# A causal convolution and soft mixture on one core: maxima of the taps carried by 32-column matmuls, and taken earlier

## Chip, core and metric

The kernel runs on one core of one Trainium2 chip. The metric is the device time of one execution in microseconds, lower is better. All data are float32.

## What is computed

The input is `x` (8 sequences of 3584 tokens, 192 channels in 8 heads of 24) and, for each token and head, 7 tap weights. The first half is a causal convolution whose 7 taps are a softmax of those weights; the second a soft mixture of 8 experts with 4 slots each.

```python
w = weight_gen - np.max(weight_gen, axis=-1, keepdims=True)     # (B, S, H, 7)
w = np.exp(w); w = w / (np.sum(w, axis=-1, keepdims=True) + 1e-09)
x_unf = x_pad[:, idx, :].reshape(B, S, K, H, group)              # 7 rows of x per token
out = np.einsum('bshk,bskhg->bshg', w, x_unf)                    # convolution
logits = out @ phi                                               # 28672 tokens x 32 slots
d = softmax of logits over the tokens;  slot_input = d.T @ out
slot_out[e] = np.maximum(slot_input[e] @ w1[e], 0.0) @ w2[e]
y = (softmax of logits over the slots) @ slot_out
```

## The kernel before

A sequence is cut into 35 groups of 104 tokens: 4 blocks of 26 tokens. Seven groups make a stage `s` (40 stages), two groups a pair `p` (140 pairs), eight pairs a unit `u`. PE, DVE, ACT and POOL each run their instructions in the order in which the kernel writes them; the main loop gives each step a planned moment (`at(t, step, ...)`), sorts by it and writes the steps in that order. `start[p]` is pair p's planned begin, with CONV = 0.8, XPOSE = 0.46, ROWS = 0.5, LOGITS = 1.5 and DISPATCH = 0.75 as planned lengths. SP issues the loads in the same list.

The steps of a pair, with the lines of the profile:

- `conv(p)`, L223, PE: 16 matmuls of 26 stationary columns (a banded matrix of taps) by 100 moving columns of x. The four blocks of a group write to four bands of 32 output partitions of one of three buffers `cv`. A float32 matmul stands in the trace as two MATMUL and two LDWEIGHTS records.
- `conv_sum` (L232, ACT) and `conv_out` (L239 reciprocal and L240 multiply, DVE) divide by the sum of the taps and write `tm`.
- `xpose(p - 3)`, L253, PE: three transposes, copied out by ACT (L258).

The steps of a stage's taps, seven pairs ahead of the stage's first convolution, in four stages' buffers `taps`:

- `tap_top(s)`, L176, DVE: maximum over the 7 taps, from 128 x 392 to 128 x 56. It waits for the load of `taps` (L169).
- `tap_rows(s)`, L182, PE: carries these maxima to the rows of x at which the taps stand. For each of the 7 tap positions q, one matmul with the 128 x 128 matrix `sel[:, q]` as stationary operand and the 128 x 56 maxima as the moving one. `sel[:, q]` links only rows and columns of the same head, that is, it has four blocks of 32 x 32. The result goes to `topP`, a part of the PSUM tile `pmx`.
- `tap_sub` (L186, DVE), `tap_exp` (L190, ACT) and `band_make` (L199, POOL, four instructions) subtract, exponentiate and lay out the banded matrices.

The steps of a unit: `logits` (L282, PE), `top` and `save` (L289, L291, L295, DVE), `newmax` (L304, PE; it writes another part of `pmx`), `newmax_out` (L309, L311, DVE), `dexp` (L315, ACT), `dturn` (L327, DVE), `dispatch` (L347, PE) and `rescale` (L355, DVE). The softmax over slots (L77 to L90) runs beside them on DVE, POOL and ACT. After the loop come the experts and the output matmuls (L609 to L670).

Stages 0 to 2 have their taps prepared in a hand-written part ahead of the loop; the other 37 in the loop.

Of the kernel before, what the change touches and what calls it, by code (L numbers as in the profile page):

```python
# [41 lines left out]
def conv_soft_moe(ctx, tc, xh, wh, phi, w1a, w1b, w2, out):  # L42
    nc = tc.nc
    V, A, G, P, SY = nc.vector, nc.scalar, nc.gpsimd, nc.tensor, nc.sync
# [72 lines left out]
    topP = pmx[:, 0:TAPS].rearrange("p (q l) -> p q l", q=KT)  # L117
# [30 lines left out]
    sel = keep.tile([128, KT, 128], F32, name="sel")  # L148
# [22 lines left out]
    tops = {}  # L171
# [7 lines left out]
    def tap_rows(s):  # L179

        for q in range(KT):
            P.matmul(topP[:, q], sel[:, q], tops[s][:, :, 0], start=True, stop=True)  # L182

    def tap_sub(s):
        r = taps[s % NTAP][:, 1].rearrange("p (b q o) -> p q b o", q=KT, o=2)
# [164 lines left out]
    def rescale(u):  # L350
# [3 lines left out]
        else:  # L354
# [13 lines left out]
                    op=ALU.mult)  # L368
    tap_top(0)
    tap_rows(0)  # L370
    for q in range(4):
        r = slice(32 * q, 32 * q + 32)
# [20 lines left out]
    for t in tms:  # L393
        V.memset(t[:, :, 0:1], 1.0)
        V.memset(t[:, :, 2 * D + 1 : 2 * D + 2], 1.0)
    conv(0)
    tap_rows(1)
    conv_sum(0)
    conv_out(0)
# [15 lines left out]
    conv_out(1)  # L415
    tap_top(2)
    tap_rows(2)
    tap_sub(2)
    tap_exp(2)
    band_make(2, 0, 14)  # L420
    band_make(2, 14, HB)
    for q in range(4):
        r = slice(32 * q, 32 * q + 32)
# [24 lines left out]
    start = [0.0]  # L448
# [7 lines left out]
    def at(t, f, *a):  # L456
        todo.append((t, len(todo), f, a))

    for p in range(first, PAIRS):
        t = start[p]  # L460
        at(t, conv, p)
        at(t + CONV + 0.1, conv_sum, p)
        at(t + CONV + 0.4, conv_out, p)
        if p >= LAG:
            at(t + CONV, xpose, p - LAG)
            at(t + CONV + XPOSE + 0.05, xpose_out, p - LAG)
        t += CONV + XPOSE
        if p in rowed:
            s = rowed[p]
            at(t - 1.2, tap_top, s)  # L470
            at(t, tap_rows, s)
            t += ROWS
            at(t + 0.1, tap_sub, s)
            at(t + 0.7, tap_exp, s)
            at(t + 1.4, band_make, s, 0, 14)
            at(t + 3.4, band_make, s, 14, HB)
    saved = {}
    for u in range(1, final + 1):
        v, p0 = u - 1, UNITS[u][0]
        t = start[p0 + LAG + 1] - LOGITS  # L480
# [5 lines left out]
        if u < final:  # L486
            t = start[p0 + LAG + 2] - 0.01
# [5 lines left out]
            t = start[p0 + UP] - DISPATCH  # L493
            at(t, dispatch, v)
            at(t + DISPATCH + 0.2, rescale, v)
    for h in range(2 * EARLY):
        t = saved[(sum(HALVES[h]) - 1) // (2 * UP)] + 1.5
# [3 lines left out]
    for s in range(NSG):  # L501
        for part in range(2):
            g = SGG * s + (SGH, SGG)[part] - 1
            t = start[g // 2] + CONV * (0.5, 1)[g % 2] + 0.01
# [97 lines left out]
    for i in range(E + E // 2):  # L602
        for q in range(4):
            r = slice(F // 4 * q, F // 4 * (q + 1))
# [32 lines left out]
    for e in range(E):  # L637
        for c in range(FC):
            q = c % 4
            P.matmul(so4[32 * q : 32 * q + 32], hT[:, c, NS * e : NS * e + NS],  # L640
                     w2_at(e, q * 2 + c // 4),
                     start=(e == 0 and c < 4), stop=(e == E - 1 and c >= 4))
# [132 lines left out]
```

## Time and profile before

| | |
|---|---|
| median of 3 runs | 432.2 us (428.71 to 448.68) |
| profiled execution | 427.8 us |
| its span, first to last instruction | 426.1 us |
| mean granted TensorE clock | 0.918 |
| PE busy (matmul records) | 378.1 us, 89% of the span |
| DVE, POOL, ACT busy | 267.6, 180.7, 164.0 us |

A line of the profile names the engine, the source line, the operation, the tiles written and read, and the number of instructions. PE is the matmul stream and PEld the weight loads; they overlap. In the timeline the first column is the start in us, the second the length of the merged piece, and brackets give the idle time ahead of it and what ended it. The ends of matmuls are modelled, so lengths hold a fixed tail of about a quarter of a microsecond.

### The profile page before, as it was taken

The page shows a single profiled execution, that of the slowest core. Times are in us where ns is not written, and L with a number is a line of the kernel's source. Part 1 is how long each engine was busy: PE and PEld are TensorE (multiplying, and loading weights), DVE is VectorE, ACT ScalarE, POOL GpSimd, SP SyncE. Part 2 cuts the span into 40 slices and gives each one's busy share as a digit, 9 for nine tenths or more (in the row PEclk, how much of TensorE's full clock was granted, in tenths as well). Part 3 has the DMA queues.
Part 4 walks back from the last instruction along what each step waited for, and adds up shares of the span by engine and source line. Part 5 has one row for each costly group of instructions (what it writes and reads, how often), then busy time and mean ns, then how long its engine had stood idle before and what let it go on. Part 6 is the DMA issues. An engine that isn't in the chain of part 4 may idle for free.

```text
span 426.1 us, 16874 instructions
## 1 busy us (share of the span) xinstructions
PE 378.1 (89%) x7184; PEld 283.5 (67%) x7184; DVE 267.6 (63%) x631; ACT 164.0 (38%) x424; POOL 180.7 (42%) x206
## 2 busy tenths in 40 slices
PE   7589999989999998989989999998989998998940
PEld 7577777867777786777868778786767665323310
DVE  5636657655766766676776766676676754877440
ACT  4224334333434434343443434434344412543420
POOL 3435454545635654653755653564753243000000
PEclk9569999979999999999999999999999999995555
DMA  5626888883464653355464464555453690699996
GB/s 149 176 75 185 269 248 233 262 253 108 137 171 120 156 166 108 108 152 167 123 175 129 113 186 132 137 143 152 113 147 94 234 361 3 266 399 401 400 398 240
DMA packets 31131, 80.85 MB, mean 190 GB/s; under 512 B 6864, under 2 KB 6992, under 8 KB 31056
## 3 DMA queue, kind: packets, MB, share of 16 engines
q1 hardware_dynamic: 31056, 79.77, 59.8%
q8 instruction: 57, 0.93, 0.9%
q14 instruction: 18, 0.15, 0.1%
HBM read 57.38 MB, written 22.36 MB: 187 GB/s over the span
## 4 chain that ended last, share of the span: by engine, by line
PE 59%; DVE 22%; DMA 6%; ACT 4%; issue 3%; SPq 2%; DVEq 0%; POOL 0%; ACTq 0%; POOLq 0%
PE pmx L182 17%; PE cv L223 15%; PE pt L253 7%; PE ls L282 7%; DVE tm L240 6%; PE ac L347 6%; DMA out<-big 6%; DVE top L176 3%; PE po L661 2%; DVE ws L239 2%; SPq L670 2%; DVE mx L289 2%; DVE LT L295 2%; ACT dd L315 2%; PE hp L609 1%
## 5 line engine op out<-in xcount | busy, mean ns | idle before, releaser
L199 POOL TENSOR_TENSOR band<-taps,mask 128x140 f32<-128x140 f32 (+2 forms) x156 | 137.8, 913 | 120.1 <-issue 91.7
L223 PE MATMUL cv<-big,band 128*26 128x100 f32 x4480 | 128.1, 255 | 3.5 <-POOL band L199 3.5
L223 PEld LDWEIGHTS cv<-big,band 128*26 128x26 f32 x4480 | 100.1, 107 | 18.6 <-issue 8.4
L182 PE MATMUL pmx<-top,sel 128*128 128x56 f32 x560 | 74.6, 288 | 20.7 <-DVE top L176 18.3
L182 PEld LDWEIGHTS pmx<-top,sel 128*128 128x128 f32 x560 | 69.8, 202 | 28.2 <-DVE top L176 24.9
L240 DVE TENSOR_TENSOR tm<-cv,ws 128x384 f32<-128x384 f32 x140 | 78.2, 559 | 15.0 <-PE pmx L182 0.5
L253 PE MATMUL pt<-ident,tm 122*128 122x122 f32 x420 | 74.9, 288 | 0.0
L258 ACT COPY cm<-pt 128x312 f32<-128x312 f32 x140 | 58.2, 417 | 13.8 <-PE pt L253 12.9
L239 DVE RECIPROCAL ws<-ws 128x16 f32<-128x16 f32 x140 | 33.6, 240 | 40.6 <-ACT ws L232 39.2
L253 PEld LDWEIGHTS pt<-ident,tm 122*128 122x128 f32 x420 | 43.3, 142 | 22.1 <-issue 20.1
L232 ACT ACTIVATE ws<-cv,eps 128x16 f32<-128x16 f32 x140 | 37.5, 268 | 52.5 <-PE cv L223 51.6
L190 ACT ACTIVATE taps<-taps 128x392 f32<-128x392 f32 x40 | 21.2, 530 | 90.8 <-DVE taps L186 90.8
L661 PE MATMUL po<-cT,so 32*128 32x442 f32 (+3 forms) x256 | 44.8, 771 | 2.8 <-DVE big L668 2.0
L186 DVE TENSOR_TENSOR taps<-taps,pmx 128x392 f32<-128x392 f32 x40 | 22.5, 563 | 35.9 <-PE pmx L182 33.0
L668 DVE COPY big<-po 128x936 f32<-128x936 f32 (+1 forms) x24 | 26.1, 1094 | 16.4 <-DMA out<-big 9.0
L661 PEld LDWEIGHTS po<-cT,so 32*128 32x128 f32 (+1 forms) x256 | 15.6, 199 | 30.8 <-ACT big L668 12.6
L668 ACT COPY big<-po 128x936 f32<-128x936 f32 (+1 forms) x24 | 21.8, 917 | 32.1 <-DMA out<-big 11.3
L79 POOL TENSOR_TENSOR LT<-LT,rm 128x576 f32<-128x576 f32 (+1 forms) x16 | 18.0, 1130 | 36.6 <-DVE rm L77 33.3
L282 PE MATMUL ls<-cm,phi_sb 128*32 128x208 f32 (+1 forms) x576 | 28.4, 336 | 0.9 <-ACT cm L258 0.9
L347 PE MATMUL ac<-tm,dt 128*32 128x193 f32 x544 | 28.0, 349 | 1.2 <-DVE dt L327 1.2
L90 POOL TENSOR_TENSOR LT<-LT,sm 128x576 f32<-128x576 f32 (+1 forms) x16 | 18.1, 1132 | 11.9 <-DVE sm L88 7.6
L282 PEld LDWEIGHTS ls<-cm,phi_sb 128*32 128x32 f32 x576 | 16.5, 109 | 8.2 <-ACT ws L232 1.3
(112 smaller groups left out, 245.2 us busy)
## 6 DMA issues: line engine op xcount, KB each, us to landing
big<-xh SPq DMA_DIRECT2D x160, 100.0 KB, 2.5
taps<-wh SPq DMA_DIRECT2D x40, 392.0 KB, 4.1
big<-xh SPq DMA_DIRECT2D x160, 75.0 KB, 3.3
out<-big SPq DMA_DIRECT2D x24, 468.0 KB, 6.4
out<-big SPq DMA_DIRECT2D x24, 442.0 KB, 6.5
big<-w SPq DMA_DIRECT2D x7, 768.0 KB, 9.1
w1a_sb<-w1a SPq DMA_DIRECT2D x8, 512.0 KB, 4.9
w1b_sb<-w1b SPq DMA_DIRECT2D x4, 512.0 KB, 6.3
```

What stands on the lines that cost most here:

```text
L182: P.matmul(topP[:, q], sel[:, q], tops[s][:, :, 0], start=True, stop=True)
L199: eng.tensor_tensor(out=w[:, :, z].rearrange("p b (a k) -> p b a k", k=k), in0=r[:, :, :, 0:k].to_broadcast([128, hi - lo, a, k]), in1=m[: ...
L223: P.matmul(cv[32 * blk : 32 * blk + T, o : o + 4 * GX], bands[s % NBAND][:, bc // 2, :, bc % 2], xb[:, :, bc * GX : (bc + 1) * GX], start= ...
L232: A.activation(wss[p], cvs[p % NCV][:, 0 : 16 * GX].rearrange("p (h w) -> p h w", w=GX)[:, :, GW:], AF.Identity, bias=eps[:, 0:1])
L239: V.reciprocal(ws, ws)
L240: V.tensor_tensor(out=tms[u % NTM][:, pr, 1 : 2 * D + 1].rearrange("p (h w) -> p h w", w=GW), in0=cv[:, :, 0:GW], in1=ws.to_broadcast([128 ...
L253: P.transpose(pt[:, i, 0:TR], tm[0:TR, pr, 1 + 128 * i : 129 + 128 * i], ident[0:TR, 0:TR])
L258: copy(cms[u][:, pr].rearrange("p i b j -> p (i b) j"), pts.pop(p).rearrange("p i (b j) -> p (i b) j", j=32)[:, :, 0:T])
L282: P.matmul(lp[32 * blk : 32 * blk + 32, 0:n, par, 0:T], phi_sb[:, 2 * par + i, :], cm[:, 0:n, 1 if i else 2 * par, blk, :], start=(i == 0) ...
L347: P.matmul(ac[32 * q : 32 * q + 32], dt[:, g, :], tm[:, g // 2, o : o + D + 1], start=(g < 4), stop=(g + 4 >= 2 * n))
L661: P.matmul(po[dst : dst + hi - lo, q % 2, 0 : n * T], so[32 * q : 32 * q + 32, lo:hi], cT[32 * q : 32 * q + 32, g0 : g0 + n, 0:T], start=T ...
L668: (V.tensor_copy if done[1] % 2 else A.copy)(ot.rearrange("p (q c) -> p q c", q=2), po[:, :, 0 : n * T])
```

## The change

Each matmul of `tap_rows` becomes four, one for each 32 columns of `sel[:, q]`, each writing its own band of 32 partitions of `topP`; all four still read all 128 rows and the same moving operand. In the loop, `tap_top` is planned 2.5 ahead of `tap_rows` instead of 1.2.

```diff
     def tap_rows(s):
         for q in range(KT):
-            P.matmul(topP[:, q], sel[:, q], tops[s][:, :, 0], start=True, stop=True)
+            for r in range(0, 128, 32):
+                P.matmul(topP[r : r + 32, q], sel[:, q, r : r + 32], tops[s][:, :, 0],
+                         start=True, stop=True)
...
         if p in rowed:
             s = rowed[p]
-            at(t - 1.2, tap_top, s)
+            at(t - 2.5, tap_top, s)
             at(t, tap_rows, s)
             t += ROWS
             at(t + 0.1, tap_sub, s)
```

The orders of ACT, POOL and SP are the same in both, as is that of PE but for the count of the matmuls. On PE, at stage 20, these stand in a row before:

```order
L182 MATMUL pmx_98<-top20_2625,sel_138 128x56 x7
L347 MATMUL ac6_2645<-tm0_91,dt6_2604 32x193 x16
L223 MATMUL cv1_95<-big_67,band0_88 26x100 x16
L253 MATMUL pt61_2686<-ident_132,tm1_92 128x122 x3
L223 MATMUL cv2_96<-big_67,band0_88 26x100 x16
```

and now (the lines of the changed kernel are one or two higher):

```order
L183 MATMUL pmx_98<-top20_3007,sel_138 32x56 x28
L349 MATMUL ac6_3086<-tm0_91,dt6_3026 32x193 x16
L225 MATMUL cv1_95<-big_67,band0_88 26x100 x16
L255 MATMUL pt61_3127<-ident_132,tm1_92 128x122 x3
L225 MATMUL cv2_96<-big_67,band0_88 26x100 x16
```

Seven matmuls with 128 output rows have become 28 with 32, and nothing else has moved. On DVE, at the same stage (`ws`, `tm`: conv_out; `rm`: softmax over slots; `dd`, `dt`: dturn), before:

```order
L239 RECIPROCAL ws61_2567<-ws61_2567 128x16
L240 TENSOR_TENSOR tm1_92<-cv1_95,ws61_2567 128x384
L77 TENSOR_REDUCE rm5_2590<-LT_65 128x17
L322 MEMSET dd_93 64x32
L324 MEMSET dd_93 32x4
L327 STREAM_TRANSPOSE dt6_2604<-dd_93 128x512
L239 RECIPROCAL ws62_2600<-ws62_2600 128x16
L240 TENSOR_TENSOR tm1_92<-cv2_96,ws62_2600 128x384
L176 TENSOR_REDUCE top20_2625<-taps0_84 128x56
```

and now:

```order
L241 RECIPROCAL ws61_2987<-ws61_2987 128x16
L242 TENSOR_TENSOR tm1_92<-cv1_95,ws61_2987 128x384
L176 TENSOR_REDUCE top20_3007<-taps0_84 128x56
L77 TENSOR_REDUCE rm5_3012<-LT_65 128x17
L324 MEMSET dd_93 64x32
L326 MEMSET dd_93 32x4
L329 STREAM_TRANSPOSE dt6_3026<-dd_93 128x512
L241 RECIPROCAL ws62_3022<-ws62_3022 128x16
L242 TENSOR_TENSOR tm1_92<-cv2_96,ws62_3022 128x384
```

The reduce of `tap_top` has moved up six rows here, past one `conv_out` and a `dturn`. In the loop it moves up two to six rows at 33 of the 37 stages, past one `conv_out` each time and at some of them past a `dturn`, a `newmax_out`, a `top` and `save` or a `rescale` too; at four stages (10, 17, 26, 33) it stays where it was.

## Prediction

> **What bounds the kernel now.** I read the page first: busy times, and the chain that ended last by engine and by line.
>
> ```profile
> PE 378.1 (89%) x7184; PEld 283.5 (67%) x7184; DVE 267.6 (63%) x631; ACT 164.0 (38%) x424; POOL 180.7 (42%) x206
> ...
> PE 59%; DVE 22%; DMA 6%; ACT 4%; issue 3%; SPq 2%; DVEq 0%; POOL 0%; ACTq 0%; POOLq 0%
> PE pmx L182 17%; PE cv L223 15%; PE pt L253 7%; PE ls L282 7%; DVE tm L240 6%; PE ac L347 6%; DMA out<-big 6%; DVE top L176 3%; PE po L661 2%; DVE ws L239 2%; SPq L670 2%; DVE mx L289 2%; DVE LT L295 2%; ACT dd L315 2%; PE hp L609 1%
> ```
>
> The changed line, L182, has the largest share of the chain: 17% of 426.1 us, 73 us for 40 rounds of work. L176 adds 3%. Then the busy times of the loop alone, and the waits in it (total us, times, longest).
>
> ```profile
> core 0: us, PE busy (x) PEld busy (x) DVE busy (x) ACT busy (x) POOL busy (x), PEclk, DMA share, GB/s
> 20.00:333.00 313.00, 292.52 (x6293) 236.55 (x6297) 205.87 (x514) 126.36 (x369) 164.63 (x180) 0.97 0.56 156
> ```
> ```profile
> DVE ws L239 <- ACT ws L232: 36.8, 51, 2.4
> DVE taps L186 <- PE pmx L182: 25.5, 26, 2.6
> PEld pmx L182 <- DVE top L176: 21.0, 25, 2.1
> PEld pmx L182 <- DVE mq L311: 2.8, 4, 0.7
> PE ac L347 <- DVE dt L327: 1.2, 3, 0.6
> ```
>
> In the loop PE is busy 292.5 of 313 us, DVE only 205.9. Nearly all that PE waits for is the maxima: 21.0 + 2.8 = 23.8 us by the weight loads' count, at 29 of 37 stages. So time taken off PE here is time taken off the loop, until DVE stands in the way.
>
> **The matmuls.** Here is one stage without a wait, and the next pair, without taps.
>
> ```profile
> 74.22 0.54 PE L253 MATMUL pt<-ident,tm 122*128 122x122 f32 x3
> 74.49 1.64 PEld L182 LDWEIGHTS pmx<-top,sel 128*128 128x128 f32 x14
> 74.59 1.67 PE L182 MATMUL pmx<-top,sel 128*128 128x56 f32 x14
> 76.19 0.89 PE L223 MATMUL cv<-big,band 128*26 128x100 f32 x32
> ```
> ```profile
> 77.02 0.53 PE L253 MATMUL pt<-ident,tm 122*128 122x122 f32 x3
> 77.48 0.89 PE L223 MATMUL cv<-big,band 128*26 128x100 f32 x32
> ```
>
> From the transposes to the convolution it is 76.19 - 74.22 = 1.97 us with the taps and 77.48 - 77.02 = 0.46 without: they cost 1.51 us. The 14 loads follow each other at (1.64 - 0.19) / 13 = 0.112 us, while a convolution's 32 records, each with more moving columns, take 0.89 in all. So loading 128 columns sets the pace, not streaming 56. What 32 columns cost is shown by neighbours: the convolution's 32 run on four bands, and less the tail of some 0.25 its starts lie within 0.64 us, 0.020 each; eight rounds of four, so a round takes some 0.088 for 100 columns. Small loads stand further on.
>
> ```profile
> 348.00 0.14 PEld L577 LDWEIGHTS pst<-phi_sb,accS 128*32 128x32 f32 x2
> 348.17 0.20 PEld L582 LDWEIGHTS psu<-selE,accS 128*64 128x64 f32 x4
> ...
> L577 PEld LDWEIGHTS pst<-phi_sb,accS 128*32 128x32 f32 x2 | 0.1, 108 | 0.0
> ```
>
> Two loads of 32 columns on one band start 0.14 - 0.108 = 0.03 apart, and four of 64 columns on two bands fit in 0.20: bands load beside each other. The 56 new records are 14 rounds of four. A round is bounded below by the load, 0.03, if streaming cost nothing, and above by four convolution records, 0.08. The convolution's round scaled to 56 columns is 0.049, and its load is hidden, as there; I take **14 x 0.049 = 0.69 us** instead of 1.51. The change of shape after the transposes is in the 0.46 already. Over 37 stages that is 37 x 0.82 = **30.3 us**. (At four stages a 128-column matmul follows and the shape changes back; under 1 us, left out.)
>
> The three stages prepared ahead of the loop are on the chain too, the first as in the loop, two at half clock, which shows in a piece twice as long:
>
> ```profile
> 13.90 3.24 PE L182 MATMUL pmx<-top,sel 128*128 128x56 f32 x14
> ...
> 22.19 3.23 PE L182 MATMUL pmx<-top,sel 128*128 128x56 f32 x14 [3.56 <-DVE top L176]
> ```
>
> Half the clock doubles what is saved, so 0.8 + 2 x 1.6 = **4.0 us**. The wait of 3.56 us stays: that part is written by hand, and its order on DVE is unchanged.
>
> **The earlier maxima.** The longest waits look like this:
>
> ```profile
> 163.18 0.56 DVE L240 TENSOR_TENSOR tm<-cv,ws 128x384 f32<-128x384 f32 x1
> 163.65 0.71 DVE L77 TENSOR_REDUCE rm<-LT 128x17 f32<-128x544 f32 x1
> 164.20 0.53 PE L253 MATMUL pt<-ident,tm 122*128 122x122 f32 x3
> 164.53 0.71 DVE L327 STREAM_TRANSPOSE dt<-dd 128x512 f32<-128x512 f32 x1
> 165.95 0.55 DVE L176 TENSOR_REDUCE top<-taps 128x56 f32<-128x392 f32 x1
> 166.56 1.64 PEld L182 LDWEIGHTS pmx<-top,sel 128*128 128x128 f32 x14 [2.05 <-DVE top L176]
> ```
>
> Moved to behind the multiply of 163.18, the reduce ends at 164.2, before the transposes: the 2.05 us go. But L327 then ends at 164.53 + 0.71 + 0.55 = 165.8, and `dispatch`, which follows the taps and reads it, would be ready at 164.66 + 0.69 = 165.35: a new wait of 0.45. There are four such places. Elsewhere the reduce passes at least one `conv_out` (0.24 + 0.56 us of DVE), and the mean wait is 21.0 / 25 = 0.84, so most end. The reduce issues nothing but itself, and no other engine's order changes, SP's and POOL's loads and bands included. At the four "mq" waits the taps still wait for L311, which ends earlier by the 0.55 of the reduce now ahead of it; 0.2 of 0.7 stays. I leave 3 of the 23.8 us: **20.8**. What the reduce delays by 0.55 is mostly `conv_out`; its readers come three pairs later, 3 x 1.29 = 3.9 us, which covers it. Without that cover each stage would lose 0.55, 20 us in all.
>
> **New waits.** The four of 0.45 on `dt`, and the three present ones (1.2 us) grow by perhaps 0.3 each: 2.7. The moved reduce may find its load not landed, and then all of DVE stands behind it.
>
> ```profile
> DMA to landing us min/median/max: 3.0/4.1/6.1
> ```
> ```profile
> 35.34 0.35 SPq L169 DMA_DIRECT2D taps<-wh  x1
> ...
> 41.91 0.55 DVE L176 TENSOR_REDUCE top<-taps 128x56 f32<-128x392 f32 x1
> ```
>
> This is the tightest stage, 6.6 us from issue to reduce; with 0.8 from the move and 1.6 from two shorter stages 4.2 are left, a wait of up to 2 us for DVE, partly covered. I allow 1.8 in all, so **-4.5**.
>
> **The clock.** After one such wait the clock fell to half for some 6 us, after another more briefly (the first row is the same work undisturbed):
>
> ```profile
> 72.09 1.51 PE L347 MATMUL ac<-tm,dt 128*32 128x193 f32 x32
> ...
> 90.26 3.24 PE L182 MATMUL pmx<-top,sel 128*128 128x56 f32 x14 [1.80 <-DVE top L176]
> 93.43 2.80 PE L347 MATMUL ac<-tm,dt 128*32 128x193 f32 x32
> ...
> 168.26 2.34 PE L347 MATMUL ac<-tm,dt 128*32 128x193 f32 x32
> ```
>
> (3.24 - 1.67) + (2.80 - 1.51) + (2.34 - 1.51) = 3.7 us. Without the waits that should go; since two equal waits had no fall, I take **3**.
>
> **Sum.** 30.3 + 4.0 + 20.8 - 4.5 + 3 = 53.6 us. The profiled execution took 427.8 us, so **374 us**. The median of the three runs is 1% above that execution, which I put into the range.
>
> **Rivals.** (a) *Starting a matmul has a price of its own.* If a record can't start faster than in the convolution, 0.020 us, the 56 take 1.12 instead of 0.69: 40 x 0.43 = 17 us are lost, **391**. Against it: a round's length there fits streaming, as it grows with the columns (32 records of L347 with 193 columns take 1.51; less a tail of 0.34, seven rounds of 0.167 are again 0.088 per hundred columns). The Trainium skill, page "TensorE: Matmul & The Clock Gate", section "Wait — 56ns, not 53.3ns?", says that starts never come closer than about 25 ns however few the columns. By it the 56 would take an estimated 1.40 us and the kernel about 402; the 0.020 of the convolution is already below it.
>
> (b) *DVE becomes the bound.* With 48 us off the loop, DVE would be busy 206 of 265 us, 78%. If its 36.8 us of waits for ACT stay and it only gains part of its 25.5 us for the taps, the loop falls by 33 instead: **391**. For it: its order is fixed, and it waits once a pair. Against it: 107 us of idle time.
>
> (c) *Slower: bands load and stream one after another*, 0.03 + 0.049 = 0.08 us for each of 56, 4.4 us a stage: 374 + 40 x 3.7 = **522**. Other gains are 19 us, 0.48 a stage, so this decides from (1.51 + 0.48) / 56 = 0.036 us per matmul on. The Trainium skill, same page, section "The mechanism", has loads overlap running matmuls only where the row groups differ, and here all use all rows. The convolution, with the same rows, runs at 0.020: the trace disagrees.
>
> (d) *Nothing measurable*: both halves hidden. PE's 93% in the loop speaks against it.
>
> **Chances.** Forecast 0.62; (a) 0.17; (b) 0.14; (d) 0.03; (c) 0.04. The low end is all waits gone and no new ones, 427.8 - 30.3 - 4.0 - 23.8 - 3.7 = 366. A round at its lower bound, 0.03, would take 40 x 14 x 0.019 = 11 us more off; with the convolution's round so near to streaming I allow 3 of them. The high end takes in (a) and (b) and the median's 1%: 391 + 1% = 395, and 3 more for new waits a good half larger than allowed. Two per cent, 8.6 us, is about what a measurement here can tell from none. Faster by over that: 0.93; within: 0.03; slower: 0.04.
>
> **What would show it.** 2240 matmul records of `tap_rows`, a stage's busy piece near 0.9 us with its tail instead of 1.67; PE's wait for the top reduce under 4 us in the loop; that of `dispatch` for L327 near 3; DVE's wait for the taps roughly halved; the loop's clock at 0.98 or more instead of 0.97, DVE's share there near 78%. I am wrong if the piece is 1.3 us or longer, or if PE in the loop waits more than 12 us.

## The result and the profile after

The changed kernel takes 396.1 us (median of four runs, 395.57 to 397.02) where the kernel before takes 430.5 (four runs, 427.91 to 448.68) in the same session: ratio 0.922, 95% interval 0.916 to 0.929. The ratio leaves out the one execution of 448.68, which stands far from the others of the same kernel. The profiled execution took 396.47 us instead of 427.8, so 31.3 us are gone, not the 53.6 that the sum gave. The time lies inside the forecast range of 363 to 398, near its upper end.

From the page of the changed kernel: busy times, and the chain that ended last by engine and by line.

```profile
PE 344.5 (87%) x8864; PEld 246.9 (63%) x8864; DVE 265.2 (67%) x631; ACT 161.3 (41%) x424; POOL 180.7 (46%) x206
...
PE 66%; DVE 11%; DMA 9%; issue 6%; ACT 3%; SPq 1%; DVEq 0%; POOL 0%; ACTq 0%; POOLq 0%
```

Then the loop of the changed kernel by itself (columns as in the row of before: window and its length, busy times, granted clock, DMA share, GB/s), and what PE waited for there (total us, times, longest).

```profile
20.00:302.00 282.00, 261.11 (x7902) 202.25 (x7903) 201.67 (x510) 123.72 (x369) 164.01 (x179) 0.98 0.62 174
```
```profile
PE cv L225 <- issue: 15.1, 16, 2.7
PE pmx L183 <- DVE top L176: 4.5, 2, 3.9
PE ac L349 <- DVE dt L329: 1.4, 4, 0.6
PE ac L349 <- issue: 1.1, 1, 1.1
PE pmx L183 <- issue: 1.1, 3, 0.5
PE ls L284 <- issue: 0.8, 2, 0.4
```

PE's work shrank and its waits for the maxima are nearly gone (of the 4.5 us, 3.9 belong to the hand-written part), yet PE is still idle for 21 of these 282 us. The largest row is new: 15.1 us ahead of convolution matmuls, "issue", which is time in which PE waits for nothing that the profile shows. The three other "issue" rows add 3.0.

Cut at the first start of the convolution of pair 2, the loop's first, and at the last start of all, the profiled executions compare so:

| us | before | after | difference |
|---|---|---|---|
| up to the convolution of pair 2 | 25.4 | 21.0 | -4.4 |
| loop | 311.8 | 284.9 | -26.9 |
| rest | 89.0 | 88.9 | -0.1 |

**What the new idle time is.** The timeline of the changed kernel at its longest stall but one:

```profile
71.80 0.58 PE L183 MATMUL pmx<-top,sel 128*32 128x56 f32 x32
...
72.19 0.68 PE L225 MATMUL cv<-big,band 128*26 128x100 f32 x19
...
74.93 0.88 PE L225 MATMUL cv<-big,band 128*26 128x100 f32 x13 [2.06 <-issue]
75.73 0.49 PEld L255 LDWEIGHTS pt<-ident,tm 122*128 122x128 f32 x3 [0.30 <-issue]
75.73 0.87 PE L255 MATMUL pt<-ident,tm 122*128 122x122 f32 x3
...
76.53 1.55 PE L225 MATMUL cv<-big,band 128*26 128x100 f32 x32
...
78.59 0.89 PE L225 MATMUL cv<-big,band 128*26 128x100 f32 x32
```

A convolution whose operands are all there stops after 19 of its 32 records. Two microseconds later it goes on, and for some 3 us after that PE runs at half speed (transposes 0.87 instead of 0.53, a convolution 1.55 instead of 0.89). A break in the middle of a step that waits for nobody points at the instructions themselves. The queue of the page that loads instructions has more packets than before; here are the rows of before and of after:

```profile
q8 instruction: 57, 0.93, 0.9%
```
```profile
q8 instruction: 70, 1.15, 1.3%
```

Each packet is 16 KB. The trace has 14,549 PE records before and 17,910 after (matmuls, weight loads, and some semaphore instructions): one packet for 256 records in both, and 13 packets more for 3,361 records more. I numbered the records from 0 in order of start, and call the time from the start of one record to that of the next a break where it is over 0.2 us. Records 193, 449, 705 and so on lie 256 apart; I call them borders. In the loop of the changed kernel 28 breaks, 25.6 us in all, stand at borders; before there is one, of 0.35 us. So PE's code seems to come in pieces of 256 records, with PE standing at the border of one until it has arrived. The packets' own times fit: in a stall PE goes on 1.2 to 1.6 us after a packet's end. The stall above ends at 74.92; the packet ran from 72.20 to 73.45.

Leaving these breaks out, the loop is 311.8 - 0.35 = 311.4 us before and 284.9 - 25.6 = 259.3 after. The difference, 52.1, is near the 49.6 that the sum held for the loop (53.6 less the 4.0 ahead of it).

### The profile page after: what moved, and what is told of

The parts are those of the page before. It is cut to its first block, busy times and chain, and to the rows that moved or that the text cites. A ratio compares the mean times of both kernels' runs of the same rounds, so it can differ in the third digit from the quotient of the medians.

```text
span 394.8 us, 20235 instructions
## 1 busy us (share of the span) xinstructions
PE 344.5 (87%) x8864; PEld 246.9 (63%) x8864; DVE 265.2 (67%) x631; ACT 161.3 (41%) x424; POOL 180.7 (46%) x206
## 4 chain that ended last, share of the span: by engine, by line
PE 66%; DVE 11%; DMA 9%; issue 6%; ACT 3%; SPq 1%; DVEq 0%; POOL 0%; ACTq 0%; POOLq 0%
PE cv L225 24%; PE pt L255 13%; DMA out<-big 8%; PE pmx L183 8%; PE ls L284 7%; PE ac L349 6%; DVE tm L242 2%; PE po L663 2%; PE hp L611 1%; PE cv L131 1%; PE so L642 1%; DVE big L670 1%; DVE mx L291 1%; DVE LT L297 1%; ACT dd L317 1%
## 5 line engine op out<-in xcount | busy, mean ns | idle before, releaser
L225 PE MATMUL cv<-big,band 128*26 128x100 f32 x4480 | 134.3, 254 | 19.0 <-issue 15.1
L225 PEld LDWEIGHTS cv<-big,band 128*26 128x26 f32 x4480 | 103.4, 106 | 36.4 <-issue 27.7
L183 PE MATMUL pmx<-top,sel 128*32 128x56 f32 x2240 | 38.2, 218 | 5.8 <-DVE top L176 4.5
L183 PEld LDWEIGHTS pmx<-top,sel 128*32 128x32 f32 x2240 | 31.5, 112 | 13.1 <-DVE top L176 5.4
```

The source lines that it names most:

```text
L183: P.matmul(topP[r : r + 32, q], sel[:, q, r : r + 32], tops[s][:, :, 0], start=True, stop=True)
L225: P.matmul(cv[32 * blk : 32 * blk + T, o : o + 4 * GX], bands[s % NBAND][:, bc // 2, :, bc % 2], xb[:, :, bc * GX : (bc + 1) * GX], start= ...
```

## The experiments

The theory: **the code supply.** PE now gets through 256 records in less time than the next piece takes to come. The rivals are given with each run. "Breaks" below means the breaks at these borders in the loop, read from the one profiled execution of each kernel.

### The two halves apart

128 columns with the early maxima, as an edit of the kernel before:

```diff
-            at(t - 1.2, tap_top, s)
+            at(t - 2.5, tap_top, s)
```

> The earlier maxima alone, matmuls of 128 columns as before. Theory S (supply of PE's code: its records come in pieces of 256, a piece is asked for only when PE enters the one ahead of it, and PE stalls where it uses up 256 records before that comes, some 4 to 5 us): with 14,500 records as before a piece lasts some 6 us, so no stall at piece boundaries (under 2 us in all), PE's wait for the maxima under 3 us, about 405 us (428 - 21 for the waits - 4 for the clock + 2 for new waits). Rival D (what is missing of the forecast gain is held back by DVE's fixed order): the waits come back elsewhere, 413 us or more.

And four matmuls of 32 columns with the maxima at their old place, as an edit of the changed kernel:

```diff
-            at(t - 2.5, tap_top, s)
+            at(t - 1.2, tap_top, s)
```

> Four matmuls of 32 columns, maxima taken as late as before. Theory S: taps of 0.69 us a stage as in the changed kernel, waits for the maxima back at some 20 us; part of them lies over piece boundaries, during which code arrives, so stalls there fall from 25 to some 12 us: 405 us. If the two costs simply add (waits as before on top of the changed kernel), 417 us. Rival D: within 2 us of the changed kernel, 396.

Early maxima alone: 402.9 us (401.35 to 408.11), ratio 0.938 [0.932, 0.943]; breaks 1.3 us. Short matmuls alone: 410.3 (409.78 to 411.73), ratio 0.957 [0.952, 0.961]; breaks 21.1 us. PE's waits with the short matmuls alone:

```profile
PE pmx L183 <- DVE top L176: 18.7, 18, 5.0
PE cv L225 <- issue: 13.5, 15, 3.0
```

| | loop, us | breaks, us | loop without breaks |
|---|---|---|---|
| before | 311.8 | 0.35 | 311.4 |
| early maxima alone | 287.2 | 1.3 | 285.9 |
| short matmuls alone | 298.7 | 21.1 | 277.6 |
| both | 284.9 | 25.6 | 259.3 |

The early maxima alone came out near the 405 forecast for them, without stalls, so DVE's order (413 or more) isn't what holds the gain back. The stalls come with the short matmuls, also where the maxima are late. There I was wrong on their size: the waits for the maxima did not cover them, they fell to 21.1 us and not to 12, and 410.3 lies between the theory's 405 and the 417 of costs that simply add. Without the breaks the halves are worth 25.5 and 33.8 us, 59.3 together; both at once give 52.1; why they overlap by 7 us isn't shown. With the breaks the short matmuls bring 13.1 us of the loop beside late maxima and 2.3 beside early ones: nearly all they save beside the early maxima is given back at the borders.

### Half as many records

Two matmuls of 64 columns, early maxima:

```diff
-            for r in range(0, 128, 32):
+            for r in range(0, 128, 64):
-                P.matmul(topP[r : r + 32, q], sel[:, q, r : r + 32], tops[s][:, :, 0],
+                P.matmul(topP[r : r + 64, q], sel[:, q, r : r + 64], tops[s][:, :, 0],
```

> Two matmuls of 64 columns (two heads) instead of four of 32; maxima early. 56 records for a stage instead of 112, 16,000 in all. Theory S: a stage's taps take some 14 rounds of 0.056 = 0.78 us (+0.09 x 37 = 3 us), the stalls at piece boundaries fall from 25 us to under 10: 383 us, faster than the changed kernel. Rival T (the stalls come from small column tiles as such, in proportion to their number): half of them stay, 387 to 390. Rival D: 399.

387.5 us (386.62 to 388.25), ratio 0.902 [0.897, 0.908], the intervals of this and the changed kernel do not overlap. Its waits on PE, and its code:

```profile
PE pmx L183 <- DVE top L176: 5.6, 4, 4.2
PE cv L225 <- issue: 2.8, 4, 1.4
PE ls L284 <- ACT cm L260: 2.1, 3, 0.9
```
```profile
q8 instruction: 61, 1.00, 1.1%
```

A stage's taps are slower than with 32 columns: 0.81 us from first to last start instead of 0.68, and 0.15 us from the last start to the next convolution instead of 0.03. Between 64 columns and the convolution's bands the shape changes once more (behind 128 columns it is 0.21). Over 37 stages that is 4.6 + 4.5 us, which is what the loop without breaks is longer: 274.9 - 6.5 = 268.4 instead of 259.3 us. But it has 15,670 records instead of 17,910, breaks of 6.5 us instead of 25.6, and wins by 8.5 us. The time is the one that rival T had, 387 to 390, and not the theory's 383; what speaks for the theory are the breaks, of which T leaves half and the theory under 10 us. The theory's time had not counted the second change of shape.

### The border is counted in records

Sixteen matmuls of one moving column (64 records) behind the first stage's taps, into PSUM that nobody reads:

```diff
+        if s == 0:
+            for i in range(16):
+                r = i % 4 * 32
+                P.matmul(pmx[r : r + 32, 410 + i : 411 + i], sel[:, 0, r : r + 32], tops[s][:, 0:1, 0], ...
```

> The changed kernel with 16 more matmuls of one moving column behind the taps of stage 0, where PE waits for data anyway: 64 records more ahead of the loop. Theory S: PE's long stalls without a releaser stand again at record numbers 193 modulo 256, thus at other places of the program than before (64 records earlier in it); their sum stays near 20 to 26 us and the time at 394 to 398 us. If the stalls belong to places in the program, they stand at 1 modulo 256 now (193 + 64).

399.1 us (396.95 to 404.91), ratio 0.926 [0.920, 0.932], a little over the 394 to 398 expected. Every later step now stands 64 records further on. Of the breaks of over 0.4 us from 24 to 300 us, 25 with 31.0 us are still at record 193 of each 256 and 4 of under 0.6 us elsewhere; in the changed kernel 22 with 23.7 us, and 5 elsewhere. A break that belonged to a step of the kernel would have moved to 257, that is, to 1 of the next 256. Its sum is larger, 33.4 us, where 20 to 26 were expected; the profiled execution was the longest of the four, 404.91 us, so only the place is read from it.

### Is it the rate, and not the number?

The early 128-column matmuls with 21 matmuls of one moving column a stage, which stand in the trace as 42 matmuls and 42 weight loads: as many records as in the changed kernel, but no work saved. First three behind each of the seven:

```diff
             P.matmul(topP[:, q], sel[:, q], tops[s][:, :, 0], start=True, stop=True)
+            for r in range(0, 96, 32):
+                P.matmul(pmx[r : r + 32, 410 + q : 411 + q], sel[:, q, r : r + 32], tops[s][:, 0:1, 0], ...
```

> The kernel with the earlier maxima alone (128 columns), and for each tap position three more matmuls of 32 columns by one moving column into an unused part of PSUM: the same number of PE records as the changed kernel, 17,900, and no work saved. Theory S (supply of code by pieces of 256 records): stalls at piece boundaries come back, 10 us or more in all where there was 1.3; with 0.3 to 0.5 us a stage for the fillers themselves (11 to 18 us) the time is 403 + 25 = 428 us or more. Without S, stalls at boundaries stay under 3 us and the time is 403 + 11 to 18 = 414 to 421.

506.9 us (504.81 to 516.08), ratio 1.177 [1.169, 1.185]: the fillers themselves were far dearer than any theory had it, so its time answers a different question. But its breaks are 0.2 us, with the changed kernel's 17,910 records and 6.13 us between borders at the median, where the theory had 10 us or more. Its timeline:

```profile
201.42 0.43 PE L182 MATMUL pmx<-top,sel 128*128 128x56 f32 x2
201.78 0.15 PEld L184 LDWEIGHTS pmx<-top,sel 128*32 128x32 f32 x6
...
201.94 0.43 PE L182 MATMUL pmx<-top,sel 128*128 128x56 f32 x2
202.30 0.15 PEld L184 LDWEIGHTS pmx<-top,sel 128*32 128x32 f32 x6
```

A round of two large and six small matmul records takes 201.94 - 201.42 = 0.52 us. Then all 21 behind the last of the seven:

```diff
             P.matmul(topP[:, q], sel[:, q], tops[s][:, :, 0], start=True, stop=True)
+        for i in range(21):
+            r = i % 4 * 32
+            P.matmul(pmx[r : r + 32, 410 + i : 411 + i], sel[:, 0, r : r + 32], tops[s][:, 0:1, 0], ...
```

> 128 columns and the early maxima, with 21 matmuls of 32 columns by one moving column (42 records) behind the last of a stage's seven, into a part of the PSUM tile that nobody reads: as many records as in the changed kernel, in another mix, and the shape changes once a stage instead of six times more as in the filler between the matmuls. Theory 'a stall comes where 256 records take PE less than about 4.5 us': the 42 records cost about 0.5 us a stage, 18 us, pieces come to a mean of 4.9 us as with 64 columns, gaps 5 to 10 us: 425 to 430 us. Rival 'a stall belongs to a piece, whatever its time': gaps near 25 us, about 446. If a start on PE has a price above 0.02 us, the 42 cost 0.84 us or more a stage and the pieces are longer, with no gaps: 435 or more.

423.6 us (422.44 to 424.66), ratio 0.984 [0.977, 0.991]; breaks 4.3 us. Its timeline:

```profile
200.94 1.64 PEld L182 LDWEIGHTS pmx<-top,sel 128*128 128x128 f32 x14 [0.23 <-DVE mq L315]
...
202.64 0.45 PEld L185 LDWEIGHTS pmx<-top,sel 128*32 128x32 f32 x42
...
202.98 0.68 PEld L227 LDWEIGHTS cv<-big,band 128*26 128x26 f32 x32
```

With the 17,910 records of the changed kernel it breaks 4.3 us instead of 25.6, and the 446 of a price per piece is out. So not the number of pieces counts, but how fast PE gets through one: the median time between borders, stalls included, is 4.83 us here and 4.55 in the changed kernel, and 6.33 before. In the changed kernel, the time of PE's work in a piece, without the break at its end, shows where the breaks begin:

| work in a piece, us | pieces | with a break of over 0.2 us |
|---|---|---|
| 3 to 3.5 | 14 | 11 |
| 3.5 to 4 | 16 | 10 |
| 4 to 4.5 | 14 | 6 |
| over 4.5 | 16 | 0 |

One more, under 3 us, had no break. (These are the pieces from 24 to 300 us.) Before, 39 of 44 pieces take 5 to 9 us.

### More work at nearly no cost

The taps' matmuls of q = 0 to 5 stream their 56 maxima twice; the second copy falls on the next q's place and is overwritten:

```diff
+                n = 2 if q < KT - 1 else 1
-                P.matmul(topP[r : r + 32, q], sel[:, q, r : r + 32], tops[s][:, :, 0],
+                P.matmul(pmx[r : r + 32, q * NBC : (q + n) * NBC] ..., sel[:, q, r : r + 32],
+                         tops[s] ... .to_broadcast([128, n, NBC]),
```

> The changed kernel, where the matmuls of taps 0 to 5 stream their 56 maxima twice, 112 moving columns; the second copy falls on the place of the next tap and is overwritten by it. No record more, PE longer at work: 12 rounds x 0.049 = 0.59 us a stage, 22 us in the loop, 0.36 a piece. Theory 'the code comes at its own pace and PE waits for it': in pieces that stall (27 of 61) the added work only fills the gap, so gaps fall from 25.6 to about 14 us and the loop grows by some 12 us, total about 408. Rival 'the gaps are a price per piece': gaps stay near 25 us and the total rises by all of it, about 418.

402.0 us (400.96 to 406.96), ratio 0.938 [0.928, 0.947]. Its taps, loop and largest break row:

```profile
199.91 1.31 PEld L184 LDWEIGHTS pmx<-top,sel 128*32 128x32 f32 x56 [0.16 <-DVE mq L296]
```
```profile
20.00:302.00 282.00, 271.92 (x7797) 217.33 (x7801) 200.09 (x502) 120.63 (x363) 163.37 (x179) 0.99 0.63 175
```
```profile
PE cv L228 <- issue: 6.3, 9, 1.3
```

The loads of a stage now spread over 1.31 us; in the changed kernel (quoted below) over 0.75. That is 0.56 us a stage more work, 20.7 in the loop. The loop grew by 286.1 - 284.9 = 1.2 us, and the breaks fell from 25.6 to 10.7. Another 2.4 us is the fall of PE's other waits over 0.3 us; the last 2 or so are spread over the other steps. The rest of the 6 us is ahead of the loop (24.2 instead of 21.0 us) and in the spread of the runs. The rival's 418, with a price per piece, is out; the theory's 408 was still too high: the breaks fell by 14.9 us, where I had reckoned with 11 or 12.

### What holds the code back

A packet of code starts some time after PE has entered the piece before it: median 1.60 us in the changed kernel, then it takes 1.08, and PE goes on about 1.41 after its end in the stalls, 4.1 us in all. Where the data queues were busy under the median in that stretch the start came after about 1.3 us, where above, about 2.0. First the loads of the experts' weights, which fall into stages 1 to 8, were spread over stages 1 to 22:

```diff
-            if part == 1 and 0 < s <= E:
-                e = s - 1
+            if part == 1 and s % 3 == 1 and s < 3 * E:
+                e = s // 3
...
```

> The changed kernel with the loads of the experts' first weights (12 of 512 KB) spread over stages 1 to 22 instead of 1 to 8. Theory S: the time in which a piece of code comes depends on the other transfers; the stalls at piece boundaries between 20 and 86 us, 11 us now in a sixth of which DMA is busiest, fall to 5 or less, stages 9 to 22 gain some: 390 us. Rival D or T: 396, nothing changes for PE.

395.8 us (393.23 to 396.76), ratio 0.921 [0.916, 0.927]: no difference from the changed kernel. The theory's 390 is missed. Breaks before 95 us fell from 11.5 to 8.5, where I had expected 5 or less, and those later grew from 14.0 to 15.1; one profiled execution of each can't tell such differences from none. The part that I had put on these loads mostly isn't theirs. The same spread with 64 columns:

> Two matmuls of 64 columns, and the loads of the experts' first weights spread over stages 1 to 22. With 64 columns 4.9 of 6.5 us of boundary stalls lie before 95 us, where those loads run. If these loads hold up the code, the stalls before 95 us fall under 1.5 us and the time to 383 us or less; if not, as the spread with 32 columns suggests (25.6 to 23.6 us), the stalls stay at 4 us or more and the time at 386 to 388.

382.4 us (381.19 to 386.5), ratio 0.891 [0.884, 0.897]: the fastest here that computes everything. Against 64 columns alone the intervals only just touch, and the breaks are 5.8 instead of 6.5 us, 3.0 of them before 95 us instead of 4.9: between the two forecasts (under 1.5, or 4 and more). The time is the one of the theory (383 or less), the breaks hardly explain it, so what the spread adds isn't settled. Then data that is really gone: no loads of x after the first two stages, so that later stages convolve the x of those two:

```diff
             if s + 2 < NSG:
-                at(t, loadx, s + 2, part)
+                pass
```

> The changed kernel without the loads of x after the first two stages (160 of its DMAs become 16; later stages convolve the x of stages 0 and 1), everything else as it is. Of the loop's 174 GB/s about 28 of 49 MB go. PE executes the same 17,910 records. Theory 'the code packet stands in line with the data packets': in the changed kernel the next piece's packet started 1.27 us after PE entered a piece where the data queues were busy under the median, 2.03 where above; with most data gone it should start near 1.0, a piece is then ready after 1.0 + 1.08 + 1.4 = 3.5 us instead of 4.1, and the gaps at piece borders fall from 25.6 to 10 us or less: about 381 us. Rival 'only the rate of records counts, the data traffic has no part': the gaps stay above 18 us and the time at 390 to 396.

381.3 us (380.28 to 383.16), ratio 0.886 [0.880, 0.893]. Its loop and its rows of waits:

```profile
20.00:302.00 282.00, 267.52 (x8142) 207.75 (x8142) 209.18 (x532) 127.55 (x385) 166.54 (x184) 0.99 0.30 95
```
```profile
PE pmx L183 <- DVE top L176: 6.1, 4, 4.7
PE cv L225 <- issue: 3.0, 5, 1.1
PE ls L284 <- ACT cm L260: 2.8, 3, 1.0
PE pmx L183 <- issue: 2.5, 2, 1.8
```

The DMA share fell from 0.62 to 0.30, the packets' median start from 1.60 to 0.87 us, the breaks from 25.6 to 8.3, 7.3 of these before 95 us, where the experts' weights still load. A packet's own time stays at 1.08 us; what moves is its start. Not all of this move is the data's doing: where there are few breaks, packets start sooner with the same data too (median 0.53 us in the kernel before, some up to 0.8 us ahead of the border's record). Compared alike, for pieces that PE entered after a break, the median start is 1.51 us in the changed kernel (28 pieces) and 1.19 here (10). The matmuls and weight loads are the same, but PE has 17,764 records, not the 17,910 expected: 146 semaphore instructions went with the loads. So data traffic delays code, and with most of it gone the breaks fall by 17.3 us. The gain of some 15 us in time isn't that alone: other waits of PE over 0.3 us grew from 5.0 to 11.4 us, and what the 146 semaphore instructions cost isn't measured apart.

## Why the prediction was right and wrong

**The matmuls: right.** The changed kernel's stage without a wait, from its timeline:

```profile
273.51 0.53 PE L255 MATMUL pt<-ident,tm 122*128 122x122 f32 x3
273.97 0.75 PEld L183 LDWEIGHTS pmx<-top,sel 128*32 128x32 f32 x56 [0.16 <-issue]
273.98 0.90 PE L183 MATMUL pmx<-top,sel 128*32 128x56 f32 x56
274.64 0.69 PEld L225 LDWEIGHTS cv<-big,band 128*26 128x26 f32 x32
274.69 0.87 PE L225 MATMUL cv<-big,band 128*26 128x100 f32 x32
```

From transposes to convolution it is 274.69 - 273.51 = 1.18 us, 1.97 before: 0.79 saved, where 0.82 was forecast. The piece with its tail is 0.90. First to last start is 0.683 us for 56 matmul records, 0.012 each, so 14 rounds of 0.049 hold. The trace has the rounds themselves: the four bands start 0.007 us apart, and the next round 0.049 after the last one began. A convolution's round takes 0.0865, so the forecast's 0.088 was right and its 0.08, from an even 0.020 a record, was not. Ahead of the loop 4.4 us went, forecast 4.0.

**Rival (a) is out.** No start price near 0.020 us exists here: with one moving column, 42 matmul records, each with its load, take 202.98 - 202.64 = 0.34 us, 0.008 each. The Trainium skill, page "TensorE: Matmul & The Clock Gate", section "Wait — 56ns, not 53.3ns?", says that starts come no closer than about 25 ns; on four bands of 32 columns these runs show a third of it. On one and the same band the starts are four times 0.008 = 0.032 us apart even here, which stays above that figure. **Rival (c) is out** as well: at 0.012 us per matmul record instead of 0.08, bands load and stream beside each other.

**The earlier maxima: right in size.** PE's wait for L176 in the loop is 0.6 us. Without the breaks, the early maxima alone brought 25.5 us beside matmuls of 128 columns, near the 20.8 + 3 of waits and clock, and 277.6 - 259.3 = 18.3 beside those of 32.

**The clock:** 0.98 in the loop, as forecast. What that brought isn't measured apart, and the stalls now cause half-clock stretches of their own, as behind the one of 74.93 above.

**New waits: the step that failed.** Those named were too dear: `dispatch` waits 1.4 us for L329 (1.2 before, up to 3.9 allowed), DVE waits once, 1.0 us, for a load. The term missed another wait altogether: 25.6 us at the borders of the code, for which it holds nothing. I counted the 1,680 matmul records that the change adds only by their time on PE's array. With their loads they are 3,360 records of code too, 0.22 MB more, and in less time. Putting the breaks in place of the failed term, with the others as forecast, closes the sum: 30.3 + 4.0 + 20.8 + 3 = 58.1, less the breaks' increase of 25.2 and 0.2 + 1.0 for the named waits, 31.7; measured were 31.3.

The page of before showed 57 packets of 16 KB, so the added code could have been counted. What it would cost could not be read there: PE has no "issue" wait in that loop, and its pieces took 6.3 us at the median. **Rival (b), DVE:** its share in the loop is 201.67 / 282.00 = 72%, not 78, and its wait for the taps did not halve, as forecast, but nearly went. Its row in the loop before, and its rows in the loop now:

```profile
DVE taps L186 <- PE pmx L182: 28.8, 27, 3.3
```
```profile
DVE taps L188 <- PE pmx L183: 2.5, 3, 1.4
DVE top L176 <- DMA taps<-wh: 1.0, 1, 1.0
```

(b)'s 391 is nearer to the measured time than the forecast's 374, but for another reason. That 396.1 us lies inside the range is luck: its upper end was set for (a), (b) and somewhat larger waits of the named kinds, and none of these came. My own sign of being wrong did come: PE is idle for 21 us in the loop, where I had set 12.

## What to carry to other kernels

Splitting a matmul into column bands buys array time with instructions, so count the records too: an edit that raises the records per microsecond can run into the supply of code, which shows as "issue" breaks in the middle of a step, at equal distances in the record count. Compare the time in which an engine gets through one piece of its code with what a piece takes to come (here 256 records, about 4.1 us beside this kernel's data traffic), and choose the split that stays above it: 64 columns beat both 32 and 128 here. Two changes that each shorten the same engine's work are to be tried together and apart, since the second may only feed the stall.

## What the runs showed of the hardware

- PE's code arrives in 16 KB packets of 256 records. Of the changed kernel's pieces with 3 to 4.5 us of work 27 of 44 end in a break, of those with more none of 16; in its loop there are 28 breaks, 25.6 us, the longest 2.99.
- Code comes later beside data: with x's loads gone the packets start 0.87 instead of 1.60 us after a piece is entered, and 1.19 instead of 1.51 where it is entered after a break. In slower kernels with the same data they start sooner too (0.53 us in the kernel before, 1.03 with the fillers at the end), and what they wait for isn't settled.
- Weight loads of 32 columns on four bands followed each other at 0.008 us, against 0.112 for loads of 128 columns.
- Changing between 128 columns and bands of 32 is dear: with six more changes there and back a stage the 14 large and 42 small matmul records, up to the next step's, start over 204.46 - 200.89 = 3.57 us instead of 202.98 - 200.94 = 2.04, some 0.25 us each. The rows at both ends of the first figure:

```profile
200.89 0.30 PEld L182 LDWEIGHTS pmx<-top,sel 128*128 128x128 f32 x2
...
204.46 1.14 PEld L350 LDWEIGHTS ac<-tm,dt 128*32 128x32 f32 x31
```

Over 40 stages that is 61 of the 83 us between the two runs with fillers. The granted clock was lower too, 0.91 from 120 us to the loop's end, against 1.00 with the fillers at the end from 120 to 300; its cause wasn't tried.
